# Rearranging the opening of a fused FFT and feed-forward kernel: queues, one fold and one column

## The chip, the cores and the metric

The kernel runs on one core of a Trainium2 chip. A core has five engines that run side by side: TensorE (matrix products, PE in the profile, with PEld its weight loads), VectorE (DVE), ScalarE (ACT), GpSimd (POOL) and SyncE (SP, which here only issues transfers). SP, ACT and POOL each issue DMA transfers in order on a queue of their own; PEq, ACTq, POOLq and SPq in the profile are the engines' sequencers. The metric is the device time of one execution in microseconds (us); less is better.

## The reference

`x` has 8 sequences of 3008 tokens with 256 features. The reference takes the real part of a two-dimensional DFT of each sequence, and feeds each token through a two-layer network with the activation h cos(h). All is in float32.

```python
def _attn_ref(x) -> np.ndarray:
    X = np.fft.fft(x, axis=1)
    X = np.fft.fft(X, axis=2)
    return X.real.astype(np.float32)
...
def _moe_ref(x, w_in, w_out) -> np.ndarray:
    h = x @ w_in
    g = h * np.cos(h)
    return (g @ w_out).astype(np.float32)
```

`w_in` is 256 x 2048, `w_out` 2048 x 256.

## The kernel before

**The computation.** The DFT over 3008 tokens is split as 47 x 64. A first half takes DFTs of length 47 over rows folded by symmetry, with a table L of twiddles; a second half takes the 64-point part with a table BJ. The DFT over the features is not applied to x: it is folded into `w_in` (products of the table CS with the raw weights `wr`, line 583, evicted to WC and WS at line 594). The main loop then runs over 8 sequences, 6 groups of output frequencies and 8 steps of the hidden dimension: products with WC and WS (line 700) into H, rounding and sine for the cosine, and products with `w_out` (line 791) into M. While sequence b is in the main loop, the first and second halves of sequence b+1 are slipped in. Only sequence 0 has nothing to hide behind; its transform, and the preparation of the weights, is the opening.

**The opening.** The order is written out by hand: each engine gets its instructions in the order of the program text, and waits in place. A transfer also waits for an earlier one whose semaphore it takes over, of which the SP and ACT queues have eight between them.

- `load_x` (lines 166 to 178) brings x of sequence 0 in four parts p, in the order 1, 2, 0, 3, on SP and, for p of 1 and 2, half on ACT. `load_row` (162 to 164) brings one more row into part 0 by two transfers of POOL. Line 258 brings L.
- Each part p is handled as two parts c = 2p and 2p + 1, so c runs 2, 3, 4, 5, 0, 1, 6, 7. `chunk(c)` (934) calls `fold(c, 0)` and `fold(c, 1)`: VectorE adds, or subtracts, mirrored columns of x into one of two buffers xf (line 299, one instruction for the even part, one for the odd), and POOL copies two columns that have no mirror (306). `first_half(c)` multiplies by L on TensorE (320 to 335) and ScalarE evicts the result to zs (346). The two buffers xf take turns, so a fold waits for the products of the part two before it.
- `store_z` (462) and `load_z` (493) send z through DRAM to lay it out anew; `second_half` (507) multiplies it by BJ into pb, and ScalarE evicts that to pq (519, 522).
- Between store and load, TensorE makes the first folded weights: `weights` (583) from CS and `wr`, in four quarters q of 512 columns. CS and quarter 0 come by POOL after part p = 2, BJ and quarter 1 by POOL after p = 0, quarters 2 and 3 by SP.
- Row 0 of WS holds the column of frequency 128 of each hidden unit, which the main loop needs spread over partitions in `wn` (line 681 uses it as a scale). For quarter 0, `take_wn` turns it with four products of one column (603), and ScalarE copies the result (614), keeps a copy of 256 values in `wrow` (616), and POOL clears the row (617). For quarters 1 to 3, `send_wn` (621) sends the row to DRAM on ACT's queue, POOL clears it (625), and `load_wn` (627) loads it back turned.
- `keep_busy` (647) gives TensorE products on constants while x is under way. `combine_w2` (666) makes sums of blocks of `w_out` on POOL in VX.

The opening's main part, with the lines that the change touches:

```python
    for p in (1, 2, 0, 3):
        for c in (2 * p, 2 * p + 1):
            chunk(c)
            first_half(c)
        store_z(p, 0, 4, both if p == 3 else (nc.sync, nc.sync))
        if p == 2:
            load_cs(nc.gpsimd)
            load_w(0, nc.gpsimd)
        elif p == 0:
            load_bj(0, 512, nc.gpsimd)
            load_w(1, nc.gpsimd)
```

After it stand `load_z`, `load_w(2)`, the weights of quarters 0 and 1, `take_wn(0)`, `send_wn(1)`, and the transfers of `w_out` and of the rest of z.

Of the kernel before, what the change touches and what calls it, by code (L numbers as in the profile page):

```python
# [27 lines left out]
NX = 96  # L28
# [101 lines left out]
def kernel(  # L130
# [7 lines left out]
    nc = tc.nc  # L138
    NB = x.shape[0]
    L_np, L2_np, B_np, CS_np = _consts()  # L140
    L_dr = nc.inline_tensor(L_np, name="dft_L")
# [17 lines left out]
    def take_x(b, p):  # L159
        xs[b, p] = spool.tile([128, XP * ND], FP, tag="xp", bufs=4, name="xp")  # L160

    def load_row():
        for r0, r1, at, by in ((0, 32, 1, 3), (31, 47, 5, 6)):
            nc.gpsimd.dma_start(out=xs[0, 0][at:NX:by, 0:ND], in_=x_r[0, r0:r1, 32, :])

    def load_x(b, p, other):
        xt = xs[b, p]
        xv = xt.rearrange("r (i d) -> r i d", d=ND)
        i0 = XP * p
        for r0, r1, at, by in ((0, 32, 0, 3), (31, 47, 2, 6)):  # L170
            lo, hi = xv[at:NX:by], xv[at + by // 2 : NX : by]
            nc.sync.dma_start(out=lo, in_=x_r[b, r0:r1, i0 : i0 + XP, :])
            if p == 0:
                other.dma_start(out=hi[:, 1:XP], in_=x_r[b, r0:r1, 63 : 64 - XP : -1, :])
            else:
                other.dma_start(
                    out=hi, in_=x_r[b, r0:r1, 64 - i0 : 64 - i0 - XP : -1, :]
                )
# [50 lines left out]
    L = cpool.tile([128, 320], FP, tag="L", name="L")  # L229
# [4 lines left out]
    def load_cs(eng):  # L234
        eng.dma_start(
            out=CS.rearrange("p (i d) -> p i d", i=2),
            in_=CS_dr.ap().rearrange("(i p) d -> p i d", p=128),
        )

    def load_w(q, eng=nc.sync):  # L240
        eng.dma_start(
            out=wr[q][:, 0:1024].rearrange("p (i f) -> p i f", i=2),
            in_=moe_w_in[:, 512 * q : 512 * q + 512].rearrange("(i p) f -> p i f", p=128),
        )

    def load_bj(c0, c1, eng=nc.sync):
        eng.dma_start(out=BJ[:, c0:c1], in_=B_dr.ap()[:, c0:c1])
# [7 lines left out]
            in_=moe_w_out.rearrange("(q p) c -> p q c", p=128)[:, 2 * f0 : 2 * f1],  # L255
        )

    nc.gpsimd.dma_start(out=L, in_=L_dr.ap())
    for p in (1, 2, 0, 3):
        take_x(0, p)  # L260
    load_row()
    for p in (1, 2, 0, 3):
        load_x(0, p, nc.scalar if p in (1, 2) else nc.sync)
    WC = cpool.tile([128, NDFF], FP, tag="WC", name="WC")
    WS = cpool.tile([128, NDFF], FP, tag="WS", name="WS")
    wn = cpool.tile([128, 16], FP, tag="wn", name="wn")
# [4 lines left out]
    def psum(name, tag="H"):  # L271
        at = tag
        if tag == "H":
            at = f"H{turn[0] % 4}"
            turn[0] += 1
        return ppool.tile([128, 512], FP, tag=at, bufs=bank[tag], name=name)
# [11 lines left out]

    xfs = {}
    xf0 = [spool.tile([128, 2 * IP * 128], FP, tag="S", bufs=3, name="xf") for _ in range(2)]  # L290
    for xf in xf0:
        nc.gpsimd.memset(xf[64:128], 0.0)

    def fold(c, e):
        lo = IP * (c % 2)
        xv = xs[0, c // 2].rearrange("r (i d) -> r i d", d=ND)[0:NX, lo : lo + IP]
        xfs[c] = xf0[c % 2]
        fv = xfs[c].rearrange("r (e i d) -> r e i d", e=2, d=128)[0:NX]
        nc.vector.tensor_tensor(
            out=fv[:, e, :, 1:128],  # L300
            in0=xv[:, :, 1:128],
            in1=xv[:, :, 255:128:-1],
            op=ALU.subtract if e else ALU.add,
        )
        if e:
            nc.gpsimd.tensor_copy(
                out=fv[:, :, :, 0].rearrange("r e i -> r i e"), in_=xv[:, :, 0:129:128]
            )


    def first_half(c):

        fv = xfs.pop(c).rearrange("r (e c) -> r e c", e=2)
        LE, LO, LE0, LO0, LM = (L[:, 64 * q : 64 * q + 64] for q in range(5))
        pz = psum("pz", "M")
        a = 128 if c == 0 else 0
        for e, (w, w0) in enumerate(((LE, LE0), (LO, LO0))):
            rows = slice(64 * e, 64 * e + 64)
            if a:
                nc.tensor.matmul(  # L320
                    pz[rows, 0:128], lhsT=w0, rhs=fv[:, e, 0:128], start=True, stop=True
                )
            nc.tensor.matmul(  # L323
                pz[rows, a:512],
                lhsT=w,
                rhs=fv[:, e, a:512],
                start=not a,
                stop=True,
                skip_group_check=True,
            )  # L330
        if a:
            nc.tensor.matmul(
                pz[64:128, 0:1], lhsT=LE0, rhs=fv[:, 1, 0:1], start=True, stop=True
            )
        nc.tensor.matmul(
            pz[64:128, a:512:128],
            lhsT=LM,
            rhs=fv[:, 1, a:512:128],
            start=True,
            stop=True,  # L340
        )
        p, q = divmod(c, 2)
        if q == 0:
            tag, n, m = ("xp", 4, XP * ND) if p in (0, 3) else ("zs", 2, 1024)
            zps[p] = spool.tile([128, m], FP, tag=tag, bufs=n, name="zs")
        nc.scalar.copy(out=zps[p][:, 512 * q : 512 * q + 512], in_=pz)
# [110 lines left out]
    def store_z(p, j0=0, j1=NJ, engs=(nc.sync, nc.sync)):  # L457
        half, q = divmod(p, 2)
        zd, zs = take_zd(0, half), zps[p][:, 0:1024]
        for e in range(2):  # L460
            p0 = 16 * e + XP * q
            engs[e].dma_start(
                out=zd[p0 : p0 + XP, 256 * j0 : 256 * j1].rearrange("i (y d) -> y i d", d=128),
                in_=zs[64 * e + 2 * j0 : 64 * e + 2 * j1, :].rearrange("y (i d) -> y i d", d=128),
            )
# [111 lines left out]
    def fold_weights(e, n, tag="M", copy=nc.scalar.copy):  # L577
        keep_weights(e, n, weights(e, n, tag), copy)
# [13 lines left out]
    def keep_weights(e, n, pw, copy=nc.scalar.copy):  # L592
        W = WS if e else WC
        copy(out=W[:, 512 * n : 512 * n + 512], in_=pw)  # L594

    def take_wn(n):
        keep_wn(n, weight_row(n))

    def weight_row(n):
        row = WS[0:1, 512 * n : 512 * n + 512]  # L600
        pw = psum("pw", "M")
        for k in range(4):
            nc.tensor.matmul(
                pw[:, k : k + 1],
                lhsT=row[:, 128 * k : 128 * k + 128],
                rhs=ones[:, 0:1],
                start=True,
                stop=True,
            )
        return pw  # L610

    def keep_wn(n, pw):
        row = WS[0:1, 512 * n : 512 * n + 512]
        nc.scalar.copy(out=wn[:, 4 * n : 4 * n + 4], in_=pw[:, 0:4])
        if n == 0:
            nc.scalar.copy(out=wrow, in_=row[:, 0:256])
        nc.gpsimd.memset(row, 0.0)

    wds = {}

    def send_wn(n):
        row = WS[0:1, 512 * n : 512 * n + 512]
        wds[n] = dpool.tile([1, 512], FP, tag="wd", bufs=3, name="wd")
        nc.scalar.dma_start(out=wds[n], in_=row)
        nc.gpsimd.memset(row, 0.0)

    def load_wn(n, eng=nc.sync):
        eng.dma_start(
            out=wn[:, 4 * n : 4 * n + 4], in_=wds[n].rearrange("o (k p) -> (o p) k", p=128)
        )  # L630
# [6 lines left out]
    ones = cpool.tile([1, 128], FP, tag="ones", name="ones")  # L637
    nc.vector.memset(VX[:, 0:512], 1.0)
    nc.vector.memset(ones, 1.0)
    wrow = cpool.tile([1, 256], FP, tag="wrow", name="wrow")  # L640
# [55 lines left out]
    def mm1(h, e):  # L696
        s, T = h.s, h.s.T
        W = WS if e else WC
        f = 2 * s.fp + h.u
# [233 lines left out]

    def chunk(c):
        fold(c, 0)
        fold(c, 1)

    both = nc.sync, nc.scalar
    copy_v = nc.vector.tensor_copy
# [3 lines left out]
    for p in (1, 2, 0, 3):  # L943
        for c in (2 * p, 2 * p + 1):
            chunk(c)
            first_half(c)
        store_z(p, 0, 4, both if p == 3 else (nc.sync, nc.sync))
        if p == 2:
            load_cs(nc.gpsimd)
            load_w(0, nc.gpsimd)  # L950
        elif p == 0:
            load_bj(0, 512, nc.gpsimd)
            load_w(1, nc.gpsimd)
    load_z(0, 0, 0, 4)
    load_z(0, 1, 0, 4, both)
    load_w(2)
    fold_weights(1, 0, "H", copy_v)
    fold_weights(0, 0, "H", copy_v)
    take_wn(0)
    fold_weights(1, 1, "M", copy_v)  # L960
    send_wn(1)
    load_wn(1)
# [30 lines left out]
    n = len(steps)  # L993
# [14 lines left out]
    pw = [weights(0, 1, both=(0,))]  # L1008
    steps[0].pq, steps[0].nb = ready[0, 0]
    for k in range(2 * n + LAG):  # L1010
# [69 lines left out]
        if k in (1, 2, 3, 4, 5):  # L1080
            e, q = ((0, 1), (1, 2), (0, 2), (1, 3), (0, 3))[k - 1]
# [50 lines left out]
```

## Time and profile before

| | us |
|---|---|
| median of 3 runs | 1926.28 |
| lowest and highest | 1925.92 and 1926.33 |
| the profiled execution, whole | 1928.33 |
| its span, first to last instruction | 1926.5 |

The profile is of one execution. Its busy table gives each engine's busy time, share of the span and number of instructions. In a timeline a row gives start, length (us), engine, line, operation, output and input, how many instructions were merged, and in brackets the idle time ahead and what ended it. The chain of waits is followed back from the last instruction, at each step to what released it. In a table by stage, each engine has its busy time and its number of instructions, then follow the clock that TensorE was granted (1.00 is full), the busy share of the DMA engines, and GB/s.

By stage, TensorE's busy time and its clock:

```profile
0.00:20.00 20.00, 15.54 (x54) 6.59 (x55) 10.17 (x18) 5.11 (x8) 10.81 (x22) 0.91 0.85 219
20.00:40.00 20.00, 19.92 (x75) 10.99 (x72) 7.61 (x15) 7.77 (x19) 4.46 (x9) 1.00 0.55 173
40.00:60.00 20.00, 20.00 (x99) 17.51 (x98) 15.40 (x29) 14.24 (x35) 14.87 (x22) 1.00 0.91 208
```

### The profile page before, as it was taken

How to read it: one execution, taken by the hardware profiler on the slowest of the kernel's cores; microseconds unless marked ns; L12 is line 12 of the kernel's file. 1: busy time of each engine (PE TensorE's matmuls, PEld its weight loads, DVE VectorE, ACT ScalarE, POOL GpSimd, SP SyncE). 2: the span in 40 equal slices, each digit the busy share in tenths (PEclk: the TensorE clock that was granted, in tenths of full speed). 3: DMA queues.
4: the chain of work that ended last, by engine and by line, in shares of the span. 5: the costliest groups of instructions: out<-in, count | busy, mean ns of one | idle time of the engine just before them, and what ended most of it. 6: DMA issues, size and time to landing. Idle time of an engine off the chain costs nothing.

```text
span 1926.5 us, 29889 instructions
## 1 busy us (share of the span) xinstructions
PE 1915.3 (99%) x9244; PEld 1676.3 (87%) x9244; DVE 1465.2 (76%) x2537; ACT 1493.6 (78%) x3362; POOL 1426.2 (74%) x1700
## 2 busy tenths in 40 slices
PE   9999999999999999999999999999999999999998
PEld 4988899888988889888898888988889888898887
DVE  5777777777777777777777777777777777788787
ACT  3777778778787787778777787778777887778775
POOL 4778768887688776887668776788867788666775
PEclk9999999999999999999999999999999999999999
DMA  7702125011240123311142112511115111100001
GB/s 200 191 24 47 37 55 127 19 41 41 68 105 20 41 44 82 86 30 36 42 111 57 38 25 44 131 37 41 28 38 143 25 41 26 41 22 15 12 15 30
DMA packets 199297, 108.68 MB, mean 56 GB/s; under 512 B 112577, under 2 KB 183407, under 8 KB 198818
## 3 DMA queue, kind: packets, MB, share of 16 engines
q1 hardware_dynamic: 195620, 103.69, 22.8%
q10 hardware_dynamic: 2958, 1.29, 0.3%
q0 software_dynamic: 560, 1.79, 0.3%
q8 instruction: 75, 1.23, 0.3%
q14 instruction: 84, 0.69, 0.1%
HBM read 69.44 MB, written 48.39 MB: 61 GB/s over the span
## 4 chain that ended last, share of the span: by engine, by line
PE 87%; DMA 4%; SPq 4%; POOL 3%; DVE 1%; issue 1%; ACT 0%; ACTq 0%; POOLq 0%; DVEq 0%
PE M L791 52%; PE H L700 30%; DMA xp<-in_x_dram 2%; PE pb L507 2%; PE pz L397 2%; SPq L208 2%; SPq L929 1%; POOL xf L374 1%; DMA nb<-nd 1%; PE pw L583 1%; SPq L215 1%; DMA xp<-xr 0%; POOL S L758 0%; DMA nd<-pq 0%; PE pz L323 0%
## 5 line engine op out<-in xcount | busy, mean ns | idle before, releaser
L758 POOL TENSOR_TENSOR S<-r 128x512 f32<-128x512 f32 (+1 forms) x383 | 475.5, 1242 | 394.8 <-DVE r L742 339.3
L738 ACT ACTIVATE r<-r 128x512 f32<-128x512 f32 (+1 forms) x768 | 477.0, 621 | 255.0 <-DVE r L732 253.5
L732 DVE SCALAR_TENSOR_TENSOR r<-r,H 128x512 f32<-128x512 f32 (+1 forms) x768 | 518.8, 676 | 196.0 <-ACT r L728 169.4
L791 PE MATMUL M<-S,VX 128*128 128x256 f32 (+1 forms) x2304 | 619.8, 376 | 0.0
L742 DVE SCALAR_TENSOR_TENSOR r<-H,r 128x512 f32<-128x512 f32 (+1 forms) x768 | 519.0, 676 | 128.3 <-ACT r L738 87.6
L791 PEld LDWEIGHTS M<-S,VX 128*128 128x128 f32 x2304 | 435.4, 190 | 71.6 <-issue 22.7
L700 PE MATMUL H<-pq,WC 128*128 128x256 f32 (+1 forms) x1536 | 453.3, 377 | 0.1
L700 PE MATMUL H<-pq,WS 128*128 128x256 f32 (+1 forms) x1536 | 450.9, 375 | 0.0
L728 ACT ACTIVATE r<-H 128x512 f32<-128x512 f32 (+1 forms) x768 | 447.9, 583 | 0.2 <-DVE H L716 0.2
L716 DVE TENSOR_TENSOR H<-ew,H 128x256 f32<-128x256 f32 (+1 forms) x768 | 325.0, 423 | 113.3 <-PE H L700 52.8
L791 PE MATMUL M<-r,w 128*128 128x256 f32 (+1 forms) x1536 | 387.6, 375 | 0.0
L681 ACT ACTIVATE H<-nb,wn 128x256 f32<-128x256 f32 (+1 forms) x766 | 366.2, 478 | 1.8 <-DVE WS L594 0.6
L712 ACT ACTIVATE ew<-H 128x256 f32<-128x256 f32 (+1 forms) x768 | 288.0, 375 | 90.7 <-PE H L700 84.8
L791 PEld LDWEIGHTS M<-r,w 128*128 128x128 f32 x1536 | 300.3, 196 | 27.6 <-issue 0.5
L700 PEld LDWEIGHTS H<-pq,WS 128*128 128x128 f32 x1536 | 290.2, 190 | 34.6 <-issue 2.7
L700 PEld LDWEIGHTS H<-pq,WC 128*128 128x128 f32 x1536 | 279.6, 190 | 44.4 <-ACT H L681 8.0
L764 POOL TENSOR_TENSOR S<-S,r 128x256 f32<-128x256 f32 (+1 forms) x383 | 276.1, 721 | 30.0
L765 POOL TENSOR_TENSOR S<-r,S 128x256 f32<-128x256 f32 (+1 forms) x383 | 275.4, 719 | 30.0
L791 PE MATMUL M<-r,VX 128*128 128x256 f32 (+1 forms) x768 | 225.2, 375 | 0.0
L791 PE MATMUL M<-S,w 128*128 128x256 f32 (+1 forms) x768 | 225.2, 375 | 0.0
L791 PEld LDWEIGHTS M<-S,w 128*128 128x128 f32 x768 | 150.3, 196 | 14.6
L791 PEld LDWEIGHTS M<-r,VX 128*128 128x128 f32 x768 | 145.8, 190 | 14.6
(91 smaller groups left out, 913.2 us busy)
## 6 DMA issues: line engine op xcount, KB each, us to landing
out_dram<-ob SPq DMA_DIRECT2D x724, 32.0 KB
xp<-in_x_dram SPq DMA_DIRECT2D x117, 128.0 KB
xp<-xr SPq DMA_DIRECT2D x112, 128.0 KB
z<-zd SPq DMA_DIRECT2D x28, 384.0 KB
xr<-in_x_dram SPq DMA_DIRECT2D x14, 752.0 KB
zd<-zs SPq DMA_DIRECT2D x98, 96.0 KB
nb<-nd SPq DMA_DIRECT2D x39, 128.0 KB
w<-in_moe_w_out_dram SPq DMA_DIRECT2D x4, 512.0 KB
```

What stands on the lines that cost most here:

```text
L681: nc.scalar.activation(out=h.H[:, 0:T], in_=s.nb[:, 0:T], func=AF.Copy, bias=0.25, scale=wn[:, f : f + 1])
L700: nc.tensor.matmul(h.H[:, 0:T], lhsT=W[:, 128 * f : 128 * f + 128], rhs=s.pq[:, e * T : e * T + T], start=False, stop=True, skip_group_che ...
L712: nc.scalar.mul(out=h.ew[:, 0:T], in_=h.H[:, 0:T], mul=2.0)
L716: nc.vector.tensor_tensor(out=h.H[:, T : 2 * T][:, ::-1], in0=h.ew[:, 0:T], in1=h.H[:, 0:T], op=ALU.subtract)
L728: nc.scalar.activation(out=r, in_=y, func=AF.Copy, bias=BIG, scale=1.0)
L732: nc.vector.scalar_tensor_tensor(out=r, in0=r, scalar=-BIG, in1=y, op0=ALU.add, op1=ALU.subtract)
L738: nc.scalar.activation(out=r, in_=r, func=AF.Sin, bias=0.0, scale=SIN_SCALE)
L742: nc.vector.scalar_tensor_tensor(out=r, in0=y, scalar=-0.25, in1=r, op0=ALU.add, op1=ALU.mult)
L758: tt(out=sv[:, 0:2], in0=qv[:, 1:2].to_broadcast([128, 2, T]), in1=qv[:, 0:4:3], op=ALU.subtract,)
L764: tt(out=sv[:, 2], in0=sv[:, 1], in1=gv[:, 0, 0], op=ALU.subtract)
L765: tt(out=sv[:, 3], in0=gv[:, 1, 0], in1=sv[:, 2], op=ALU.add)
L791: nc.tensor.matmul(acc[key][m // 2][:, 256 * (m % 2) : 256 * (m % 2) + T], lhsT=w, rhs=a, start=first, stop=s.fp == 7, skip_group_check=True,)
```

## The change

Six things change, all in the opening.

- L is loaded by ScalarE's queue, ahead of its transfers of x, and only its 96 used rows; POOL loaded 128.
- `load_row` moves from ahead of `load_x` to after part p = 1 in the loop, still on POOL.
- CS and quarter 0 of the weights are loaded by SP right behind x, no longer by POOL after p = 2.
- `fold` takes the engine as an argument; the odd fold of part 7 runs on POOL. The column copies of parts 6 and 7 run on ScalarE, the others stay on POOL.
- `first_half` uses 96 rows of xf and L, and POOL no longer clears rows 64 to 127 of the two buffers.
- `take_wn` and its helpers go. Quarter 0 takes the way of the others: `send_wn(0)`, `load_wn(0)`; `wrow` is copied by VectorE. `load_w(2)` moves behind that on SP.

```diff
--- before.py
+++ after.py
@@ -255,12 +255,13 @@
             in_=moe_w_out.rearrange("(q p) c -> p q c", p=128)[:, 2 * f0 : 2 * f1],
         )
 
-    nc.gpsimd.dma_start(out=L, in_=L_dr.ap())
+    nc.scalar.dma_start(out=L[0:NX], in_=L_dr.ap()[0:NX])
     for p in (1, 2, 0, 3):
         take_x(0, p)
-    load_row()
     for p in (1, 2, 0, 3):
         load_x(0, p, nc.scalar if p in (1, 2) else nc.sync)
+    load_cs(nc.sync)
+    load_w(0)
     WC = cpool.tile([128, NDFF], FP, tag="WC", name="WC")
     WS = cpool.tile([128, NDFF], FP, tag="WS", name="WS")
     wn = cpool.tile([128, 16], FP, tag="wn", name="wn")
@@ -288,30 +289,28 @@
 
     xfs = {}
     xf0 = [spool.tile([128, 2 * IP * 128], FP, tag="S", bufs=3, name="xf") for _ in range(2)]
-    for xf in xf0:
-        nc.gpsimd.memset(xf[64:128], 0.0)
-
-    def fold(c, e):
+
+    def fold(c, e, eng=nc.vector):
         lo = IP * (c % 2)
         xv = xs[0, c // 2].rearrange("r (i d) -> r i d", d=ND)[0:NX, lo : lo + IP]
         xfs[c] = xf0[c % 2]
         fv = xfs[c].rearrange("r (e i d) -> r e i d", e=2, d=128)[0:NX]
-        nc.vector.tensor_tensor(
+        eng.tensor_tensor(
             out=fv[:, e, :, 1:128],
             in0=xv[:, :, 1:128],
             in1=xv[:, :, 255:128:-1],
             op=ALU.subtract if e else ALU.add,
         )
         if e:
-            nc.gpsimd.tensor_copy(
+            (nc.scalar.copy if c > 5 else nc.gpsimd.tensor_copy)(
                 out=fv[:, :, :, 0].rearrange("r e i -> r i e"), in_=xv[:, :, 0:129:128]
             )
 
 
     def first_half(c):
 
-        fv = xfs.pop(c).rearrange("r (e c) -> r e c", e=2)
-        LE, LO, LE0, LO0, LM = (L[:, 64 * q : 64 * q + 64] for q in range(5))
+        fv = xfs.pop(c).rearrange("r (e c) -> r e c", e=2)[0:NX]
+        LE, LO, LE0, LO0, LM = (L[0:NX, 64 * q : 64 * q + 64] for q in range(5))
         pz = psum("pz", "M")
         a = 128 if c == 0 else 0
         for e, (w, w0) in enumerate(((LE, LE0), (LO, LO0))):
@@ -593,29 +592,6 @@
         W = WS if e else WC
         copy(out=W[:, 512 * n : 512 * n + 512], in_=pw)
 
-    def take_wn(n):
-        keep_wn(n, weight_row(n))
-
-    def weight_row(n):
-        row = WS[0:1, 512 * n : 512 * n + 512]
-        pw = psum("pw", "M")
-        for k in range(4):
-            nc.tensor.matmul(
-                pw[:, k : k + 1],
-                lhsT=row[:, 128 * k : 128 * k + 128],
-                rhs=ones[:, 0:1],
-                start=True,
-                stop=True,
-            )
-        return pw
-
-    def keep_wn(n, pw):
-        row = WS[0:1, 512 * n : 512 * n + 512]
-        nc.scalar.copy(out=wn[:, 4 * n : 4 * n + 4], in_=pw[:, 0:4])
-        if n == 0:
-            nc.scalar.copy(out=wrow, in_=row[:, 0:256])
-        nc.gpsimd.memset(row, 0.0)
-
     wds = {}
 
     def send_wn(n):
@@ -933,7 +909,7 @@
 
     def chunk(c):
         fold(c, 0)
-        fold(c, 1)
+        fold(c, 1, nc.gpsimd if c == 7 else nc.vector)
 
     both = nc.sync, nc.scalar
     copy_v = nc.vector.tensor_copy
@@ -945,18 +921,19 @@
             chunk(c)
             first_half(c)
         store_z(p, 0, 4, both if p == 3 else (nc.sync, nc.sync))
-        if p == 2:
-            load_cs(nc.gpsimd)
-            load_w(0, nc.gpsimd)
+        if p == 1:
+            load_row()
         elif p == 0:
             load_bj(0, 512, nc.gpsimd)
             load_w(1, nc.gpsimd)
     load_z(0, 0, 0, 4)
     load_z(0, 1, 0, 4, both)
-    load_w(2)
     fold_weights(1, 0, "H", copy_v)
     fold_weights(0, 0, "H", copy_v)
-    take_wn(0)
+    copy_v(out=wrow, in_=WS[0:1, 0:256])
+    send_wn(0)
+    load_wn(0)
+    load_w(2)
     fold_weights(1, 1, "M", copy_v)
     send_wn(1)
     load_wn(1)
```

## The prediction

> **What bounds the kernel now.** I read the page's busy table first, then the chain of waits, then the opening alone.
>
> ```profile
> span 1926.5 us, 29889 instructions
> PE 1915.3 (99%) x9244; PEld 1676.3 (87%) x9244; DVE 1465.2 (76%) x2537; ACT 1493.6 (78%) x3362; POOL 1426.2 (74%) x1700
> ```
>
> TensorE works without a hole from about 10 us to the end, and the change leaves its main loop alone. So the time moves by as much as the opening's end moves. The chain of waits in the first 32 us (start, length, what):
>
> ```profile
> 1.53 7.36 DMA xp<-in_x_dram
> ...
> 14.99 0.36 POOL CS L235
> ...
> 15.68 0.60 POOL wr L241
> ...
> 16.95 0.45 PE pz L320 x4
> ...
> 18.01 0.70 POOL wr L241
> 18.71 0.69 POOL xf L306
> ...
> 20.59 1.07 PE pz L323 x3
> 21.67 0.07 PE pz L335 x2
> 21.73 3.63 PE pw L583 x8
> 25.36 0.98 PE pw L603 x8
> 26.34 1.93 PE pw L583 x4
> ```
>
> The reader is to see three things: the first half ends at 21.73; GpSimd's issue of weight transfers (L235, L241) stands in the chain ahead of its column copies (L306); and then come 3.63 + 0.98 + 1.93 us of weight work before the first second-half product (pb, L507, at 28.09).
>
> GpSimd's own rows in the timeline, and those of line 666, show what it does and what is not listed as busy:
>
> ```profile
> 16.39 1.10 POOL L306 COPY xf<-xp 96x8 f32<-96x8 f32 x2
> 17.43 0.58 POOL L247 DMA_DIRECT2D BJ<-dft_B  x1
> 18.01 0.71 POOL L241 DMA_DIRECT2D wr<-in_moe_w_in_dram  x1
> 18.71 1.29 POOL L306 COPY xf<-xp 96x8 f32<-96x8 f32 x2
> ...
> 30.25 0.52 POOL L625 MEMSET WS<- 1x512 f32 x1 [2.85 <-DMA wd<-WS]
> 35.70 1.42 POOL L666 TENSOR_TENSOR VX<-w 128x256 f32<-128x256 f32 x2 [4.94 <-DMA w<-in_moe_w_out_dram]
> ```
>
> ```profile
> L666 POOLq MODIFY_POOL_CONFIG  x2: 1/1/1, 30.7 to 30.8; - x2
> ```
>
> Line 666 is GpSimd's first TENSOR_TENSOR. Directly ahead of it stands a pair MODIFY_POOL_CONFIG, which readies GpSimd's code for that kind of instruction; what follows lies in an idle gap of 4.94 us that a transfer is said to end. Memsets, copies and transfers before it needed none. In the changed kernel's compiled order the one unnamed GpSimd instruction of this sort stands ahead of the new fold of part 7, GpSimd's new first TENSOR_TENSOR.
>
> The clock matters too (stage; busy PE, PEld, DVE, ACT, POOL; granted clock):
>
> ```profile
> 7.07:10.49 3.42, 1.41 (x4) 0.20 (x3) 1.37 (x3) 0.00 (x0) 0.79 (x2) 1.00 1.06 255
> 10.49:13.90 3.41, 3.41 (x11) 1.50 (x11) 3.08 (x5) 0.59 (x1) 0.55 (x1) 0.50 1.10 264
> 13.90:17.31 3.41, 2.69 (x21) 1.28 (x19) 3.04 (x5) 1.76 (x3) 2.90 (x5) 1.00 0.67 164
> ```
>
> A stage of 3.41 us in which TensorE was busy for 1.41 us was followed by one at half clock; a full one was followed by full clock.
>
> **The change part by part.**
>
> *Twiddles by ScalarE, no clearing.* Off GpSimd go one issue (0.69 us, L258) and two memsets (1.83 us, L292), at 1.2 to 4.8 us; GpSimd then waited for x until 9.11, so this is worth nothing, covered by the landing of x. ScalarE gets one issue (its own take 0.62 to 0.81) ahead of its x transfers. The first fold's data then land between 0.7 us later (issue delay) and 0.9 us earlier (GpSimd's queue took about 90% of one microsecond of the DMA engines in the stretch from 3 to 8 us, by the queue rows); I take 0. Matmuls on 96 rows instead of 128 save nothing: a product over 1 row (L538) and one over 128 (L700) both take 0.54 for two passes.
>
> *One row of x later.* Its two issues (0.51 each) move behind part 3's column copy, to 9.9 and 10.4. These same transfers took 5.4 and 5.8 us to land; the shortest landing of a GpSimd transfer is 3.2 (CS). So the row is there between 13.6 and 16.2. Part 0's fold started at 14.85 before. I take 16.2, since it is the same transfer and the queues are as full (DMA share 1.1 in 10.49:13.90): VectorE's parts 0, 1, 6 and even 7 then run from 16.2 at 0.60 each, to about 20.5.
>
> *Weights behind x on SP.* Two issues (0.75, 0.72) leave GpSimd between 14.93 and 16.39, where they held up part 0's copy by about 0.7 us. On SP they follow the last x issue (12.73), ahead of the first store of z (14.92), which has slack. The 0.77 MB follow x and land near 19, needed at 21.7. Gain 0.7 us for part 0, used up here by the late row.
>
> *Column copies on ScalarE for parts 6 and 7.* Each is some 0.2 us (L614, 128x4, took 0.16; L616, 1x256, 0.40). But ScalarE works in order: part 7's copy stands behind part 6's 0.59 us eviction, which waits for part 6's products. Before, those products ran back to back (20.59 follows 20.54). Now TensorE waits about 0.1 + 0.59 + 0.2 = 0.9 us between parts 6 and 7.
>
> *Last odd part on GpSimd.* The nearest row is L415: 128x508, 1267 ns, against VectorE's 0.6. In front of it on GpSimd stand the copies of parts 0 and 1 (16.2 to 17.6, each lengthened to some 0.65 beside VectorE), BJ 0.58, wr 0.71, so the pair is reached at 19.0. How long it keeps GpSimd is bounded by 0 and 4.94 us, the whole gap in which it was hidden. I take 4.9: in the gap the weight's transfer moved its last packets near 35.1 and the instruction began at 35.70, so load and transfer ended close together or the load a little earlier. It was covered before; here nothing covers it. Ready at 23.9, fold done at 25.2. TensorE has then had work for about 1.0 us of the stage 20.73:24.14 (3.41 us from 17.31), less than 1.41, so the next stage, to 27.56, goes at half clock. Part 7's odd products, 0.57 at full clock, take 1.15: the first half ends at 26.35 instead of 21.73.
>
> The Trainium skill (GPSIMD Engine Reference, section 2.1, Instruction dispatch) says that the first call after such a load pays about 6 us, measured 5.95, with no profile instruction to show for it. The gap of 4.94 contradicts that size here, if not the mechanism. By 5.95 the fold would end at 26.2, the clock would stay low to 30.97, and the time would come to about 1932.9.
>
> *First column through DRAM.* Four small products, eight in the profile at two passes each, leave TensorE (0.98, L603). Weight work is then 3.63 + 1.93 = 5.56 us. From 26.35, 1.21 us at half clock do 0.60 of it, the other 4.96 end at 32.5. z could still set this: its weight load began 5.93 us after the first half's end (27.66), so z lands within 3.25 (its issue) to 5.93 us of it; the upper end gives 32.3, just hidden. The new round trip: a row store took 1.15 us (29.01 to SP's release at 30.16). Behind its wait on SP stands wr 2, 1.6 us later than before, needed some 3 us after it lands. ScalarE's first use of wn is about 5 us away.
>
> **The sum.** pb at 32.5 against 28.09: +4.4 us, after which all moves together. The profiled execution took 1928.33 us (span 1926.5 and 1.83 around it) and would become 1932.7; the median of the runs, 2.05 below it, goes from 1926.28 to 1930.7.
>
> **The rivals.**
>
> 1. *The load is short or hidden.* For it: no row shows it busy. Then the copies on ScalarE set the end: parts 6 and 7 finish at about 23.4 with a late row, 22.5 with an early one, and the missing L603 gives back 0 to 1.05. Time 1926.0 to 1928.0, say 1927.2.
> 2. *The load is longer in traffic.* The same 256 KB took 3.2 us (CS) in a quiet stretch and 4.3 (BJ) in a full one. At that ratio 4.94 becomes 6.6, the fold ends at 26.9, half clock lasts to 30.97, pb is at 35.1: 1933.3. Against it: the traffic ends near 22.
> 3. *Faster.* x lands 0.4 us or more earlier without GpSimd's transfers, TensorE starts before 9.5, is busy more than half of 7.07:10.49 and keeps full clock. With an early row and no load to pay for, the first half ends at 20.4, and with L603 gone the time is 1924.0. It decides only if the pair costs under 2 us; L323's wait of 2.01 us at the start speaks for room, the gap of 4.94 against it.
>
> **How the numbers follow.** Forecast 0.60 (its own range 1928.5 to 1932.5), rival 2 0.18, rival 1 0.15, rival 3 0.07. The range 1926.0 to 1934.0 reaches over rivals 1 and 2. A difference of 0.2% (3.85 us, so 1922.4 and 1930.1) is about what a measurement of this kernel tells from no change. Slower: three quarters of the forecast and all of rival 2, 0.63. Faster, the better part of rival 3: 0.05. The rest, 0.32, is within 0.2%.
>
> **What would show it.** Right: a MODIFY_POOL_CONFIG pair near 19 us, an idle gap of some 5 us before GpSimd's 96x508 TENSOR_TENSOR, TensorE waiting for it with PEclk falling to 0.5 after 24, pb near 32.5. The row: part 0's fold waiting for DMA until 16. ScalarE's copy of part 7 right behind an eviction. Wrong, if GpSimd's fold starts as soon as part 1's products end, if TensorE's first product moves by over 0.7 us, or if a difference arises after 40 us.

## The result, and the profile after

| | us |
|---|---|
| changed kernel, median of 9 runs (lowest to highest) | 1930.14 (1929.1 to 1935.68) |
| kernel before, beside it, median of 9 runs (lowest to highest) | 1926.28 (1925.65 to 1927.55) |
| ratio, with its 95% interval | 1.0026 (1.0016 to 1.0036) |
| profiled execution of the changed kernel, whole, and its span | 1930.73, 1928.9 |

By the medians the change costs 3.9 us, and the forecast was 1930.7. The ratio stands for 5.0 us: unlike a median it is raised by the changed kernel's three longest runs (1933.36 to 1935.68), which are also the three with the lowest mean granted clock (0.995 and 0.996, the others 0.997 to 0.999). The trace shows that the largest term of the forecast's sum, GpSimd held up by its configuration change, did not happen. First the page's span and busy table of the changed kernel:

```profile
span 1928.9 us, 29869 instructions
PE 1914.6 (99%) x9236; PEld 1676.1 (87%) x9236; DVE 1464.0 (76%) x2537; ACT 1493.5 (77%) x3362; POOL 1422.7 (74%) x1694
```

TensorE has eight records fewer (four products of two passes) and is still 99% busy, so the loss lies where it waits, or goes at half clock. Its chain of waits through the opening (start, length, what):

```profile
10.49 4.84 DMA xp<-in_x_dram
...
15.62 0.65 POOL xf L305
...
16.34 0.40 PE pz L319 x2
...
19.22 0.04 ACT zs L345
...
19.70 0.21 ACT xf L305
...
19.96 1.08 PE pz L322 x4
...
21.14 0.59 ACT zs L345
21.72 0.11 ACT xf L305
...
23.37 6.65 PE pw L582 x12
```

Three new links are in it: the transfer of the row of x up to 15.33, and twice an eviction on ScalarE (L345) with the column copy (L305) behind it. GpSimd's fold, the forecast's main link, is not in it. Its row, from GpSimd's timeline, and the pair's, from the view of line 298 (count, shortest/median/longest in ns, first and last start):

```profile
19.21 1.70 POOL L298 TENSOR_TENSOR xf<-xp 96x508 f32<-96x508 f32 x1 [1.11 <-PE pz L334]
```

```profile
L298 POOLq MODIFY_POOL_CONFIG  x2: 45/47/49, 18.1 to 18.1; - x2
```

The pair stands at 18.1, and the fold begins at 19.21, right as the products before it (18.95 + 0.23 us) set the buffer free. Whatever the pair costs lies inside that wait of 1.11 us. The fold ends at 20.9 and TensorE's last column starts at 21.88, behind ScalarE's copy. By stage (busy PE, PEld, DVE, ACT, POOL; granted clock):

```profile
19.10:22.52 3.42, 1.87 (x13) 0.81 (x11) 0.68 (x2) 1.37 (x4) 1.70 (x1) 1.00 0.54 182
22.52:25.93 3.41, 3.41 (x8) 1.41 (x5) 0.00 (x0) 0.59 (x1) 0.00 (x0) 0.50 0.17 39
```

The holes around the two ScalarE copies leave TensorE 1.87 of 3.42 us busy, and the stage behind them goes at half clock. That one caused the other is not shown (see the last section). The half clock falls on the weight products: 6.71 us for what takes 5.42 at full clock.

The main loop's first product into M starts at 46.15, against 44.40 in the recorded execution of before. From there on the distance stays between 1.67 and 1.75 us up to the last product.

### The profile page after: what moved, and what is told of

Read it like the earlier page. It is cut to its first block, busy times and chain, and to the rows that moved or that the text cites. A ratio compares the mean times of both kernels' runs of the same rounds, so it can differ in the third digit from the quotient of the medians.

```text
span 1928.9 us, 29869 instructions
## 1 busy us (share of the span) xinstructions
PE 1914.6 (99%) x9236; PEld 1676.1 (87%) x9236; DVE 1464.0 (76%) x2537; ACT 1493.5 (77%) x3362; POOL 1422.7 (74%) x1694
## 3 DMA queue, kind: packets, MB, share of 16 engines
q10 hardware_dynamic: 3072, 1.41, 0.3%
## 4 chain that ended last, share of the span: by engine, by line
PE 89%; DMA 4%; SPq 3%; POOL 2%; DVE 1%; issue 1%; ACT 0%; ACTq 0%; DVEq 0%; POOLq 0%
PE M L767 53%; PE H L676 31%; DMA xp<-in_x_dram 2%; PE pb L506 2%; PE pz L396 2%; SPq L208 1%; SPq L905 1%; PE pw L582 1%; DMA xp<-xr 1%; POOL xf L373 1%; SPq L215 0%; PE pz L322 0%; DMA nb<-nd 0%; POOL S L734 0%; DVE r L718 0%
```

## The experiments

Theory N says that the late row, ScalarE's copies and the half clock that the idle time brings set the time. Theory F is the forecast. Each traced time is that of one execution. All differences are against the changed kernel or against before, as each heading says.

### What before looks like at its median

Before's recorded execution lies 2 us above its median, so the unchanged kernel was run once more.

> The kernel before, unchanged, once more. Its recorded execution (1928.33 us) lies 2 us above its median, and TensorE ran at half clock there from 10.49 to 13.90, inside the first half. Theory A: that half clock is the 2 us; an execution with full clock there ends its first half near 20 us instead of 21.73, starts the first second-half product near 26 instead of 28.09, and has a span near 1924.5. Theory B: the 2 us lie elsewhere (main loop or tail); then the first half ends near 21.7 here too whatever the clock.

It took 1926.81 us, with full clock from 5.87 to 1920.75. TensorE's timeline:

```profile
15.41 0.45 PE L320 MATMUL pz<-xf,L 128*64 128x128 f32 x4
...
17.92 1.50 PE L323 MATMUL pz<-xf,L 128*64 128x512 f32 x5 [0.23 <-POOL xf L306]
...
19.06 1.07 PE L323 MATMUL pz<-xf,L 128*64 128x512 f32 x3
...
20.12 3.70 PE L583 MATMUL pw<-wr,CS 128*128 128x512 f32 x8
...
26.55 1.05 PE L507 MATMUL pb<-BJ,z 128*128 128x128 f32 x8
```

Theory A holds. The first half ends at 20.2 instead of 21.73, the first second-half product starts at 26.55 instead of 28.09, and the main loop at 42.87 instead of 44.40: the recorded execution had lost 1.53 us to its half clock. This one is the yardstick from here on. Against it the changed kernel's main loop starts 3.28 us late, and the stretch from the last product into M to the end is 0.63 us longer (8.69 against 8.06): 3.9 us in all, as in the medians.

### Undoing the late row, the copies, both, and the fold

Four edits of the changed kernel. In `e1_row_early` the row goes back ahead of `load_x`:

```diff
     for p in (1, 2, 0, 3):
         take_x(0, p)
+    load_row()
...
-        if p == 1:
-            load_row()
-        elif p == 0:
+        if p == 0:
```

> The changed kernel with the one row of x issued ahead of all other x again, everything else as changed. Theory N (the late row, ScalarE's column copies and the half clock that the idle brings are the loss; the pair MODIFY_POOL_CONFIG is covered): part 0's fold follows part 5's at about 13.5 us instead of 15.51, TensorE's idle of 1.71 us before part 0 goes, the two idles of 0.78 before parts 6 and 7 stay; the first half ends near 21.7 instead of 23.3; time 1927 to 1928.5. Theory F (the forecast: the pair and the fold on GpSimd set the end): the fold's place in time hardly matters, 1929.5 to 1930.5.

In `e2_cols_vector` the column copies of the last part go to VectorE:

```diff
-            (nc.scalar.copy if c > 5 else nc.gpsimd.tensor_copy)(
+            (nc.vector.tensor_copy if c > 5 else nc.gpsimd.tensor_copy)(
```

> The changed kernel with the column copies of parts 6 and 7 on VectorE instead of ScalarE, row late as changed. Theory N: the two idles of 0.78 us go; part 7's odd products then wait for GpSimd's fold (19.2 to 20.9), the first half ends near 22 instead of 23.3; if TensorE is then busy enough for the clock to stay full another 1.7 us are saved; time 1926.5 to 1929. Theory F: no change, 1929.5 to 1930.5.

`e3_row_and_cols` has both edits:

> The changed kernel with both: the row early and the column copies of parts 6 and 7 on VectorE. Theory N: all three idles go, the clock stays full after 14 us, the first half ends at 20 to 20.5 and GpSimd's fold of 1.70 us, from the end of part 1's products, becomes what part 7 waits for; time 1924 to 1926, below both kernels. Theory F: 1929.5 to 1930.5.

In `e4_fold_vector` the odd fold of part 7 goes back to VectorE:

```diff
-        fold(c, 1, nc.gpsimd if c == 7 else nc.vector)
+        fold(c, 1)
```

> The changed kernel with the odd fold of part 7 on VectorE again, everything else as changed. Theory N: part 7 waits for ScalarE's column copy and not for the fold, so nothing changes: first half's end within 0.3 us of 23.3, time 1929 to 1931; the pair MODIFY_POOL_CONFIG goes back in front of the sums of w_out. Theory F: the pair and the 1.70 us fold go from the path, 1926 to 1927.

| kernel | median (lowest to highest) | ratio to before, interval | part 0 starts | last column starts | first M product | last M product to end |
|---|---|---|---|---|---|---|
| before again | 1926.81, one run | | 15.41 | 19.06 | 42.87 | 8.06 |
| changed | 1930.14 (1929.1 to 1935.68) | 1.0026 (1.0016 to 1.0036) | 16.34 | 21.88 | 46.15 | 8.69 |
| row early | 1928.38 (1927.31 to 1929.81) | 1.0009 (1.0000 to 1.0017) | 14.42 | 21.25 | 43.95 | 8.71 |
| copies on VectorE | 1928.92 (1928.31 to 1931.94) | 1.0014 (1.0006 to 1.0023) | 16.20 | 21.01 | 43.82 | 8.88 |
| both | 1928.19 (1927.5 to 1931.41) | 1.0011 (1.0002 to 1.0020) | 14.34 | 19.15 | 41.80 | 8.89 |
| fold on VectorE | 1931.5 (1929.75 to 1933.13) | 1.0025 (1.0015 to 1.0036) | 16.79 | 22.32 | 48.13 | 8.25 |

The last four columns are from the traces; the median of before beside the last four is 1926.38. The first two kernels come out in theory N's ranges and not in theory F's. Theory F falls with the last line: with GpSimd's fold gone nothing is gained, and both waits for ScalarE stand as they were. TensorE's timeline of that kernel:

```profile
20.40 1.08 PE L322 MATMUL pz<-xf,L 96*64 96x512 f32 x4 [0.78 <-ACT xf L305]
22.32 1.97 PE L322 MATMUL pz<-xf,L 96*64 96x512 f32 x4 [0.78 <-ACT xf L305]
```

In this execution two stages, 6.8 us, went at half clock, and the twelve weight products took 7.66 us; that is why its first M product is the latest of the six. Theory N's own figures are missed here too: the first half ends at 24.34, not within 0.3 us of 23.3, and 1931.5 lies above its range.

With the other one undone, the row and the copies cost each about 2 us of the main loop's start in the traces (43.82 and 43.95 against 41.80, all three at full clock). The two do not add up: without the 1.65 us of its half clock (1.29 in the weight products, 0.36 in the last column) the changed kernel would start its main loop at about 44.5, an estimate from its own rows, and that is 2.7 us after 41.80. By the medians, undoing both takes back 1.95 of the 3.9 us.

The kernel with both undone starts its main loop a full 1.07 us before the yardstick, and yet it is not faster than before. Its trace shows where the lead goes. TensorE's timeline there:

```profile
52.99 1.13 PE L507 MATMUL pb<-BJ,z 128*128 128x128 f32 x8 [0.75 <-DMA z<-zd]
```

The second group of the second half waits for the second load of z, and the lead over the yardstick shrinks from 1.07 to 0.1 us at that place. The end, 8.89 us against 8.06, turns it into a loss of 0.7 us (spans of 1925.7 and 1925.0). This profiled execution (1927.5) was the fastest of the eleven; what the others lost is not shown. So the expectation of 1924 to 1926 was missed.

### One part of the change alone

Four kernels made from before. `e7_column_only` takes the first column through DRAM:

```diff
-    load_w(2)
...
-    take_wn(0)
+    copy_v(out=wrow, in_=WS[0:1, 0:256])
+    send_wn(0)
+    load_wn(0)
+    load_w(2)
```

> Before, with the first column through DRAM alone (four products and two copies fewer, one short store and one short load on the queues more). Theory N (the loss of the change lies in the late row, the column copies and the idle that they bring): 1925.4 to 1926.4, that is 0 to 1 us faster, as the four products of 0.98 us fall away. Rival C (the short load stands on SP ahead of the last weights and the second stores and loads of z, and makes the next z late): 1926.8 to 1928, with TensorE waiting for z from DRAM at the second half's second group near 50 us.

`e8_weights_sp_only` loads CS and quarter 0 on SP behind x:

```diff
+    load_cs(nc.sync)
+    load_w(0)
...
-        if p == 2:
-            load_cs(nc.gpsimd)
-            load_w(0, nc.gpsimd)
-        elif p == 0:
+        if p == 0:
```

> Before, with the cosine table and quarter 0 of the weights behind x on SP's queue alone instead of on GpSimd's. Theory N: 1925.8 to 1926.8, no difference, since both land before the first half ends. Rival: they delay x's last parts or land late, the weight fold waits for DMA and the time is 1927 to 1928.5.

`e10_fold_pool_only` puts the odd fold of part 7 on GpSimd, and leaves its column copy there too:

```diff
-        fold(c, 1)
+        fold(c, 1, nc.gpsimd if c == 7 else nc.vector)
```

> Before, with the odd fold of the last column alone on GpSimd. Theory F (the prediction's: configuration change and fold hold TensorE up): 1930 to 1931. Theory N (the change is hidden, the fold of 1.3 to 1.8 us ends at most 0.6 us after the column before it, and GpSimd's closing drain comes 0.45 us later as in the changed kernel): 1926.6 to 1927.8.

`e11_row_late_only` moves the row behind part 1:

```diff
-    load_row()
...
+        elif p == 1:
+            load_row()
```

> Before, with the row of x behind part 1's stores alone. Theory N: part 0 starts 0.9 to 2 us later with TensorE idle ahead of it, 1927.2 to 1928.6. Rival (the forecast's first rival, that the late row is covered): 1926.2 to 1926.8.

| kernel | median (lowest to highest) | before beside it | ratio, interval | first M product | last M product to end |
|---|---|---|---|---|---|
| column through DRAM | 1927.36 (1926.32 to 1928.61) | 1926.54 | 1.0002 (0.9993 to 1.0011) | 41.83 | 7.97 |
| weights on SP | 1927.19 (1926.44 to 1927.65) | 1926.54 | 1.0001 (0.9993 to 1.0010) | 43.66 | 8.01 |
| fold on GpSimd | 1928.2 (1926.93 to 1929.08) | 1927.07 | 1.0004 (0.9995 to 1.0013) | 45.27 | 7.69 |
| late row | 1927.1 (1926.16 to 1927.68) | 1927.07 | 1.0000 (0.9992 to 1.0009) | 44.23 | 7.68 |

No part by itself makes a difference that the medians can tell (an interval here is as wide as 1.7 us to each side); the traces tell more. In microseconds the first two medians lie in the rivals' ranges, the other two between the ranges, and none in theory N's; but before was itself 0.3 to 0.8 us slower beside these runs than in the result.

*Column.* The main loop starts 1.04 us before the yardstick, as the four products are gone. Then, as in the kernel with both undone, the second half's second group waits for z from DRAM: it starts at 52.69, and 0.66 us go back there. Some 0.5 us more go near 903 and near 1733 us, for reasons that are not shown, and the end lies level with the yardstick. So the wait that rival C named is there, and it brings the part to nothing rather than to a loss. Its reason is not shown: `load_wn(0)` and the wait for it stand on SP ahead of the second stores and loads of z, but SP has issued the last of these loads by 46.14, against 46.97 in the yardstick, where nothing waits for it. SP's timeline in the two, this kernel's first:

```profile
42.56 3.58 SPq L493 DMA_DIRECT2D z<-zd  x4
```

```profile
42.04 4.93 SPq L493 DMA_DIRECT2D z<-zd  x4
```

*Weights on SP.* This execution had its half clock in the same place as before's recorded one (10.46 to 13.87), and its main loop started 0.74 us earlier than there, a lead that it kept to the last M product.

*Fold.* GpSimd's timeline, and VectorE's folds in the view of line 299:

```profile
18.77 0.69 POOL L306 COPY xf<-xp 96x8 f32<-96x8 f32 x1
19.51 1.26 POOL L299 TENSOR_TENSOR xf<-xp 96x508 f32<-96x508 f32 x1
```

```profile
L299 DVE TENSOR_TENSOR xf<-xp x15: 675/677/1982, 9.2 to 19.3; 96x508 f32<-96x508 f32 x15
```

The fold follows the copy before it without a pause (18.77 + 0.69 = 19.46), the pair at 19.4 between them, 1 ns each. The column copy behind the fold ends at 21.36, and TensorE waits 0.80 us for it. In the change this copy is on ScalarE; there it stands behind the eviction, and TensorE waits 0.78. This execution had half clock from 10.54 to 13.95, as before's recorded one had, so that one and not the yardstick is its measure: against it the main loop starts 0.87 us later. Beside GpSimd's fold VectorE's, begun at 19.3, took 1.98 us instead of 0.68. The Trainium skill (GPSIMD Engine Reference, section 1, Specifications) says that GpSimd shares its memory interfaces with VectorE and that instructions of VectorE with two inputs in memory contend for them; this row agrees. In the changed kernel GpSimd's fold was the longer one, 1.70 us beside VectorE's 0.68.

*Row.* Without the row's transfers ahead of it, x lands earlier: TensorE's first product starts at 8.55, against 10.03 in the yardstick. The late row then makes part 0 wait, but only to 15.08:

```profile
15.08 0.40 PE L319 MATMUL pz<-xf,L 128*64 128x128 f32 x2 [0.48 <-POOL xf L305]
```

In the changed kernel it was 16.34, as the row landed at 15.33 instead of 14.07. Most of that is a later issue: x landed later there, GpSimd came to the row later, and its second transfer was issued at 10.49 instead of 9.55. The transfer took 4.84 us instead of 4.52, so the 0.77 MB of CS and quarter 0, which share the DMA engines with it in the changed kernel, can account for 0.3 us at most. Why x landed later is not shown; in the five traces with the changed kernel's order of loads the first product starts between 8.95 and 9.60.

Although part 0 starts 0.33 us before the yardstick, the main loop starts 1.36 us after it, among other things because part 6 waits 0.80 us for GpSimd's column copies; the shorter end (7.68) takes 0.4 us of that back. The median shows no loss.

### The configuration change by itself

In `e6_reload_first` GpSimd adds a cleared tile to itself right behind its first memset, so that the pair has nothing to hide in:

```diff
     nc.gpsimd.memset(xm, 0.0)
+    nc.gpsimd.tensor_tensor(out=xm, in0=xm, in1=xm, op=ALU.add)
```

> After, with one add of two arrays on GpSimd (a cleared tile added to itself) right behind its first memset: it brings the configuration change of GpSimd to the kernel's first microseconds and shows its length by itself, between the end of the memset and the start of the add. Forecast of the prediction (F): about 5 us. Theory N: at most 1.2 us, as in the changed kernel's trace (18.13 to 19.21). Time as the changed kernel, 1929 to 1931, by both.

GpSimd's timeline and the view of the added line:

```profile
0.74 0.12 POOL L355 MEMSET xm<- 128x32 f32 x1 [0.29 <-POOLq L1094]
0.94 0.24 POOL L356 TENSOR_TENSOR xm<-xm 128x32 f32<-128x32 f32 x1
```

```profile
L356 POOLq MODIFY_POOL_CONFIG  x2: 11/11/11, 0.8 to 0.8; - x2
```

Memset's end to the add's start is 0.08 us, with the pair in it. Theory F's 5 us are refuted at the point itself. (The one run took 1932.79, above the 1929 to 1931 of both theories, with three stages of half clock, 17.81 to 28.05.) The gap of 4.94 us in before's trace, in which the forecast saw the load, was the wait for the transfer of `w_out` that the row names. The kernel with the fold alone on GpSimd settles that: there the pair stands at 19.4, no pair stands ahead of line 666, and the gap is there all the same. GpSimd's timeline:

```profile
36.14 1.42 POOL L666 TENSOR_TENSOR VX<-w 128x256 f32<-128x256 f32 x2 [4.50 <-DMA w<-in_moe_w_out_dram]
```

### Filling the holes

`e9_filled` puts products that nobody reads into TensorE's idle stretches of the changed kernel:

```diff
             chunk(c)
+            if c in (0, 6, 7):
+                keep_busy({0: 4, 6: 1, 7: 1}[c], "M", 512)
             first_half(c)
```

> After, with unread products on TensorE put into the idle stretches: four of 128x512 ahead of part 0, one ahead of each column of part 3. They lengthen no wait (0.45 us each against 1.94 and twice 0.78 us of idle time). Theory N, whose last term is the half clock that the idle brings: no half clock between 7 and 1915, the twelve weight products 5.4 us instead of 6.71, median 1928.4 to 1929.4, slowest run below 1931. Rival (the half clock falls there by chance of its phase, whatever TensorE does): median 1929.7 to 1930.5 and single runs up to 1935 as in the changed kernel.

The median was 1930.72 (1930.37 to 1934.16), ratio 1.0022 (1.0013 to 1.0031). TensorE's timeline:

```profile
14.51 3.70 PE L623 MATMUL pd<-VX 128*128 128x512 f32 x8
18.14 0.45 PE L319 MATMUL pz<-xf,L 96*64 96x128 f32 x4
```

The fillers were sized by one record, but a product is two passes: four took 3.70 us instead of 1.8 and put part 0 back by 1.8 us. In the trace the clock is as theory N has it: full to the end of the main loop, with 5.42 us for the weight products. The first M product starts at 46.15, the same as without fillers, so the half clock was worth about as much as the 1.3 us by which the first half ends later. The times are not: the median and the slowest run both miss theory N's figures, and the rival's median is missed by 0.2 us. So whether the idle time brings the half clock, or where its stages happen to begin, stays open, and the run gives no price for a well-sized filler.

### What costs nothing, together

`e12_best` is before with those parts alone that had shown no cost: the twiddles on ScalarE's queue, 96 rows without clearing, CS and quarter 0 on SP. Of these only the last had been run alone.

> Before, with those parts of the change alone that cost nothing in the runs: twiddles by ScalarE's queue, no clearing and 96 partitions, cosine table and quarter 0 of the weights behind x on SP. Theory N: first product near 9.4 instead of 10.0, main loop 0.5 to 0.8 us earlier, 1925.5 to 1926.3. Rival (what starts earlier is given back where the second half waits for z from DRAM, as in the kernel with the first column through DRAM alone): 1926.3 to 1927.3.

The median was 1927.51 (1927.04 to 1928.08), ratio 1.0001 (0.9993 to 1.0010). The first product starts at 9.44 and the main loop at 42.42, 0.45 us before the yardstick, and the lead is still 0.50 at the last M product: nothing is given back at z, where the rival had it. The end is 8.76 us long instead of 8.06, and takes the gain back. The median lies above both ranges of the expectation. Nothing tried here beats before.

## Why the prediction was right in time and wrong in its reason

**The pair holds GpSimd for 4.9 us: wrong.** This is the step that failed, in *Last odd part on GpSimd*. The forecast read an idle gap as the length of what stood in front of it, although the row named a transfer as the end of the wait. The pair took 0.08 us at most where it stood bare. The Trainium skill's 6 us for the first call to freshly loaded code (GPSIMD Engine Reference, section 2.1, Instruction dispatch) are not seen either: the fold comes 1.1 us behind the pair, and 0.1 us where nothing was waited for. The prediction's own mark decides it: "Wrong, if GpSimd's fold starts as soon as part 1's products end". It did. A second mark is met too, "if a difference arises after 40 us": the end of the program is 0.63 us longer, a term that the sum did not have. The fold's own length was mis-sized too, 1.70 us instead of 1.27, without effect.

**The late row: right, its size 0.7 us too large.** Forecast 13.6 to 16.2, and 16.2 taken; the row landed at 15.33, part 0's fold began at 15.51, and its products at 16.34, 0.93 us behind the yardstick. Part 0's and part 1's folds then follow one another on VectorE as forecast.

**ScalarE's copies: right in mechanism, half counted.** Forecast 0.9 us between parts 6 and 7; the waits are 0.78 us, but there are two: part 6's copy also stands behind an eviction. From part 0's start to the first column of part 3 the changed kernel needs 3.62 us, the yardstick 2.51; between the two columns 1.92 against 1.14.

**The half clock: right in size, by a rule that does not hold.** Forecast 24.14 to 27.56, because the stage ahead would have 1.0 us of work, less than 1.41. It came from 22.52 to 25.93, behind a stage with 1.87, and cost 1.29 us in the weight products and 0.36 in the last column. A stage with 1.41 us of work was followed by full clock in another run (last section), so the forecast had no rule to go by.

**The first column: right on TensorE, incomplete behind it.** From the weight products to pb the kernels with full clock and without the four products need 5.3 to 5.5 us against 6.43, as forecast. That TensorE would then wait for the second load of z was not seen; in the changed kernel the main loop is late enough to hide that, in the two of them that start it before the yardstick it took back 0.7 and 1.0 us.

**Twiddles, weights on SP: as forecast.** The first product moved from 9.95 to 9.36 (10.03 in the yardstick), where the forecast allowed 0.7; weights on SP alone brought the main loop 0.74 us forward, where it said 0.7.

**The sum and its base.** Rival 1 described the mechanism that took place and put the end of parts 6 and 7 at 23.4; it was 23.3. Its time, 1927.2, was 2.9 us low: it had no half clock in the weight products (1.29) and nothing at the end of the program (0.63), and its base was wrong as well. Like the forecast, it was made against an execution that had itself lost 1.53 us to half clock in the first half, and then laid on the median, near which the yardstick has none. That execution was also not "without a hole from about 10 us": TensorE waited 0.72 us ahead of 16.95 and 0.26 ahead of 19.45. Against the yardstick the change's bill, from one execution of each, is:

| term | us |
|---|---|
| part 0 starts late | +0.93 |
| part 0's start to part 3's first column (folds one by one, ScalarE's copy) | +1.11 |
| first to second column of part 3 (ScalarE's copy) | +0.78 |
| last column, at half clock | +0.36 |
| weight products to pb: half clock +1.29, four products less -0.98, rest -0.2 | +0.11 |
| pb to the main loop, and the main loop | -0.04 |
| end of the program | +0.63 |
| sum (1928.9 - 1925.0) | +3.9 |

That the forecast hit 1930.7 is thus chance: 4.4 us made of a wait that didn't exist stand for 3.9 us of several small ones.

## What to carry to other kernels

An idle gap says how long something was waited for, and not how long the instruction at its end takes; before a stall is built on it, the named releaser should be ruled out. A small copy moved to an engine that works in order can cost the eviction it stands behind, at every place where it stands (0.78 us, twice, here). Two changes that each delay the same path need not add up. A recorded execution can be 1.5 us off its own median by where the half clock fell, so terms of that size need a second execution to stand on.

## What the hardware showed

*The clock's stages.* They are 3.41 us long, and where they begin differs from execution to execution of the same program (full clock from 7.07 and half clock from 10.49 in before's record; full clock from 5.87, and no half clock before the program's end, in its second). The Trainium skill (TensorE: Matmul & The Clock Gate, Part 1) says the same of the window, 3413 ns and free-running. It gives half clock after an idle window; here it followed windows in which TensorE had products for 1.41 us (before's record), 1.87 us (the changed kernel) and 2.12 us (the kernel with the fold on VectorE). But the busy share alone is not the rule. In the kernel with the fold on VectorE, 1.86 us were followed by full clock, 2.12 by half:

```profile
15.24:18.65 3.41, 1.86 (x14) 1.37 (x16) 2.69 (x5) 0.27 (x2) 2.48 (x4) 1.00 0.87 257
18.65:22.06 3.41, 2.12 (x12) 0.78 (x9) 2.18 (x4) 1.73 (x4) 0.00 (x0) 1.00 0.71 233
22.06:25.47 3.41, 3.15 (x8) 1.37 (x9) 0.00 (x0) 0.79 (x3) 0.00 (x0) 0.50 0.04 11
```

And in `e12_best` a window with as little work as the one that preceded half clock in before's record, 1.41 us by four records, was followed by full clock:

```profile
5.98:9.39 3.41, 1.41 (x4) 0.34 (x2) 0.75 (x2) 0.00 (x0) 0.71 (x2) 1.00 1.09 255
9.39:12.81 3.42, 3.37 (x15) 1.69 (x16) 3.42 (x6) 1.05 (x2) 1.49 (x3) 1.00 1.05 248
```

What decides is not shown.

*A pause of GpSimd at a fixed place of its program.* The end of the program is longer in some kernels; the closing instructions of GpSimd in the trace (two DRAINs with a clearing of semaphores between them) show a part of it. The instruction records of all kernels give this:

| GpSimd instructions in all | kernels | from the first of the last two DRAINs to the end | pause |
|---|---|---|---|
| 2244 | fold on VectorE | 0.57 | none |
| 2247 | changed, row early, copies on VectorE, both, filled | 1.01 to 1.02 | 0.32 us behind the clear |
| 2248 | pair by itself, what costs nothing | 0.85 to 0.86 | 0.32 us ahead of the clear |
| 2251 to 2255 | before (twice), and the four with one part alone | 0.57 to 0.58 | none |

In both middle rows the pause stands ahead of the same instruction by count, the 2245th. The one program with fewer has no pause, and in longer ones this instruction comes before the closing ones, where a pause would be covered. By these counts the 0.43 us by which this stretch is longer in the changed kernel come from the six GpSimd instructions that it leaves out net (2253 to 2247); no run varied the count alone. The other 0.2 of the 0.63 us is not explained; the kernel with the fold on VectorE has it too, without a pause (8.25 against 8.06). What GpSimd does in the pause is not shown.
